# Order of three GpSimd subtractions, one first product and one small batch of matmuls in a fused attention and two-MLP kernel

## The chip, the cores and the metric

The kernel runs on one core of a Trainium2 chip. That core has TensorE (PE; its weight loads are shown apart, as PEld), VectorE (DVE), ScalarE (ACT), GpSimd (POOL) and SyncE (SP), which issues the DMAs. Each engine runs its own instructions in the order in which they stand, and waits on semaphores for the others. The metric is the time of one execution in microseconds on the device.

## The reference, cut to what matters

Three parts follow each other. With B = 4, H = 8, S = 512, 32 state rows per head and D = 64:

```python
a = softmax(x @ state.T / 8);   xread = a @ state
a2 = softmax(state @ x.T / 8);  sread = a2 @ x
x = concat(xread, sread)                      # 4 x 544 tokens, 512 wide
h = x @ w_in                                  # 512 -> 2048
x = softplus(h) @ w_out                       # 2048 -> 512
x = (silu(x @ w_gate) * (x @ w_val)) @ w_out2 # 512 -> 1536 -> 512
```

All of it is float32 in the reference; weights arrive as float64 words.

## The kernel before, in words

A float32 operand is split into a high float32r part (ACT) and a low part, whole minus high (POOL for most, DVE for some); every product is three matmuls: high by high, low by high, high by low (`mm3`, line 89). A weight tile of float64 words is first made float32 in steps: `size` (ACT, line 132), `head` (DVE, line 136), `tail` (two DVE instructions, lines 143 and 146).

The first MLP goes over the 2048 hidden columns in 4 chunks of 512. The attention read isn't formed: for each chunk c and batch b, `m` is the state times the chunk's w_in (`m_mm`, line 374, PE tile `pm`; high part on ACT, line 378; low part on DVE, line 92). A **unit** is (chunk, batch, 128 hidden columns): 16 units per chunk, 64 in all, numbered in that order, so that unit 9 is chunk 0, batch 2, tile 1. Each unit has these steps:

- first product `p1` (PE tile `ph_b_ft`, from `aT` and `m`, 6 matmuls),
- softplus twice on ACT: high part `h_b_ft` (line 404) and whole `C_b_ft` (line 407),
- low part `l_b_ft` = C - h on POOL (`g_low`, line 92),
- second product `p2` (PE tiles `py_b_0` to `py_b_3`, from `wo`, `h`, `l`: 4 times two matmuls with h and one with l).

`h`, `C` and `l` have three buffers each. The first product runs four units ahead of the second (LAG = 4). After the fourth unit of a batch, the four `py` go to `yacc` (DVE, and ACT in chunk 0). The state tokens (`s1`, line 505, PE tile `ps`: four matmuls with plain float32 operands) go beside this, and weights for the second MLP are converted in between.

Two things set the order. The table ORDER is a list of steps, written out by hand, for the attention and for the units up to the second product of unit 8 (`P8`) and the first of unit 12 (`p12`); there `p9` is a first product, `sp9` the two softplus, `gl9` the low part, `P9` a second product, `mh7` and `ml7` the high and low part of an `m`. From unit FIRST = 9 on a loop takes over: per step n it runs `p2` of unit n, the hooks of kind "pe", `p1` of unit n + 4, the softplus of unit n + 3 and the hooks of the other engines. M_STEPS gives the steps of a chunk at which the next chunk's four `m` batches are made; the "pe" hooks of a step also hold `s1`. The framework adds the waits and picks the buffers and PSUM banks. In the rows, a name such as `py_2_0` has lost its chunk number.

Of the kernel before, what the change touches and what calls it, by code (L numbers as in the profile page):

```python
# [31 lines left out]
)  # L32

FIRST = 9
# [3 lines left out]
def attention_moe_moe2_kernel(  # L38
# [44 lines left out]
    def bank(tag, name):  # L83
        return psum.tile([P, 512], F32, tag=tag, bufs=BUFS[tag], name=name)

    def mm3(o, a, b, first, last, **k):

        for i, (s, t) in enumerate(((0, 0), (1, 0), (0, 1))):
            nc.tensor.matmul(o, a[s], b[t], start=first and i == 0, stop=last and i == 2, **k)  # L89
# [322 lines left out]
    def p1(u):  # L412
        c, b, ft = u
        ps = bank("h", f"ph{c}_{b}_{ft}")
        f = slice(ft * P, (ft + 1) * P)
        for par in range(NPAR):
            mm3(
                ps, [mt[c, b, par][:, i, f] for i in range(2)], [aT[b, par][:, i, :] for i in range(2)],
                par == 0, par == NPAR - 1,
            )  # L420
        n = f"{c}_{b}_{ft}"
        sp[u] = Softplus(
            ps, work.tile([P, 512], F32, tag="C", name=f"C{n}"), work.tile([P, 512], F32R, tag="GH", name=f"h{n}")
        )

    def g_low(u):
        l = work.tile([P, 512], F32R, tag="GL", name="l%d_%d_%d" % u)
        low(nc.gpsimd, l, sp[u].g, sp[u].h)
        gT[u] = (sp[u].h, l)
# [5 lines left out]
    def p2(u):  # L435
        c, b, ft = u
        if ft == 0:
            for dt in range(KT):
                yps[dt] = bank("y", f"py{c}_{b}_{dt}")
        t = gT.pop(u)  # L440
        for dt in range(KT):
            mm3(yps[dt], [wo[c, ft].out[:, i, dt * P:(dt + 1) * P] for i in range(2)], t, ft == 0, ft == FT - 1)

    def y_add(c, b, dt):
        if (b, dt // 2) not in yacc:
            yacc[b, dt // 2] = slot([P, 2, 512], F32, "yacc", f"yacc{b}_{dt // 2}")
        v = yacc[b, dt // 2][:, dt % 2, :]
        if c == 0 and dt % 2:
            nc.scalar.activation(v, yps[dt], AF.Copy)
        elif c == 0:  # L450
            nc.vector.tensor_copy(v, yps[dt])
        else:
            nc.vector.tensor_tensor(out=v, in0=yps[dt], in1=v, op=ALU.add)  # L453
# [193 lines left out]


    LAG = 4
    M_STEPS = (9, 12, 15, 19)  # L650
    with tc.manual_schedule(engines={ENG.PE}):
        units = [(c, b, ft) for c in range(NCK) for b in range(B) for ft in range(FT)]
        NU = len(units)
# [3 lines left out]
        def first_load(key):  # L657
            if key == "st":
                nc.sync.dma_start(out=st, in_=st_d)
            elif key[0] == "w":  # L660
                win[0, int(key[1])] = piece_win(0, int(key[1]))
            elif key[0] == "o":
                wo[0, int(key[1])] = piece_wo(0, int(key[1]))
            else:
                (load_xt if key[0] == "x" else load_xn)(int(key[1]), int(key[2]))
# [11 lines left out]
        def do(names):  # L677
            for name in names.split():
                key = name.rstrip("0123456789")
                k = int(name[len(key):])  # L680
                if key in STEPS:
                    getattr(todo[k], STEPS[key])()
                elif key[0] in "io" and key[1:] in PIECE:
                    getattr((win if key[0] == "i" else wo)[0, k], PIECE[key[1:]])()
                elif key == "mm":
                    m_mm(0, k, 0, "m")
                    m_mm(0, k, 1, "y" if k < 2 else "h")
                elif key in BATCH:
                    BATCH[key](0, *divmod(k, 2))
                elif key == "st":  # L690
                    st_turn(k)
                elif key == "so":
                    st_out(k)
                elif key == "p":
                    p1(units[k])
                elif key == "sp":
                    sp[units[k]].high()
                    sp[units[k]].whole()
                elif key == "gl":
                    g_low(units[k])  # L700
                elif key == "P":
                    run(k, "load")
                    p2(units[k])
                elif key[0] == "y":
                    y_add(*units[k][:2], "abcd".index(key[1]))
                elif key == "jab":
                    win[1, k].size()
                elif key == "jhd":
                    win[1, k].head()
                elif key == "jtl":  # L710
                    win[1, k].tail()
# [3 lines left out]
        def at(n, kind, fn, *args):  # L715
            hooks.setdefault((n, kind), []).append((fn, args))

        def run(n, kind):
            for fn, args in hooks.get((n, kind), ()):
                fn(*args)  # L720
# [15 lines left out]
        for c in range(NCK):  # L736
# [5 lines left out]
            for i, (store, make, key) in enumerate(pieces):  # L742
                n, late = n0 + i // 2 * FT + i % 2, 2 - 2 * (i % 2)
# [3 lines left out]
            if c + 1 < NCK:  # L747
                for b, i in enumerate(M_STEPS):
                    at(n0 + i, "pe", m_pair, c + 1, b)
# [41 lines left out]
        with tc.manual_schedule(engines={ENG.DVE, ENG.SP, ENG.Activation, ENG.Pool}):  # L791
            for key in LOADS.split():
                first_load(key)
            for names in ORDER:
                do(names)
            room[0] = "m"
            for n in range(FIRST, NU):
                run(n, "load")
                if True:
                    u = units[n]  # L800
                    p2(u)
                    run(n, "pe")
                    if n + LAG < NU:
                        p1(units[n + LAG])
                nx = units[n + LAG - 1] if n + LAG - 1 < NU else None
                if nx:
                    sp[nx].high()
                    sp[nx].whole()
                last = u[2] == FT - 1
                run(n, "dve0")  # L810
                for dt in range(2) if last else ():
                    y_add(u[0], u[1], dt)
                run(n, "act")
                if nx:
                    g_low(nx)
                run(n, "pool")
                for dt in range(2, KT) if last else ():
                    y_add(u[0], u[1], dt)
                run(n, "dve1")
                run(n, "act1")  # L820
                run(n, "pool1")
            for n in range(NU, NU + FT + 1):
                for kind in ("act", "dve0", "pool"):
                    run(n, kind)
# [11 lines left out]
        for k, j in enumerate(range(len(EARLY), 3 * NF)):  # L836
            n, half = divmod(k, 2)
# [128 lines left out]
```

## Time and profile before

| what | value |
|---|---|
| time, median of 3 runs | 754.24 us (753.07 to 755.08) |
| the profiled execution: its own time | 753.34 us |
| its span, first to last instruction | 751.6 us |
| mean granted TensorE clock, share of full speed | 0.992 |
| PE busy | 722.4 us, 96% |
| DVE, POOL, ACT busy | 433.4 (58%), 385.1 (51%), 321.8 us (43%) |

The span is what the trace covers; 1.74 us of the profiled execution's time lie around it. A row of the timeline gives the start, the time to the last end, the engine, the line, and written tile <- read tiles; "[0.82 <-ACT m L378]" says how long the engine sat idle before it, and for whom. Consecutive matmuls overlap, so the pace of PE is read from start to start. "x16" in a row of a small or plain float32 batch counts records, which may be two for a matmul.

### The profile page before, as it was taken

To read this page: it belongs to the slowest core of one execution; us is meant where nothing else is said; L and a number is where in the kernel's file an instruction comes from. 1 tells how busy PE (TensorE), PEld (TensorE's weight loads), DVE (VectorE), ACT (ScalarE), POOL (GpSimd) and SP (SyncE) were. 2 spreads that over 40 slices of the span, in tenths; PEclk is the share of its full clock that TensorE was granted. 3 is DMA by queue.
4 is the path that set the end of the run, shared out by engine and by line. 5 is a ranking of instruction groups with operands and counts; after the bars stand their busy time and mean duration, and the time that the engine had idled before them with its cause. 6 is when DMAs were issued, how large, how long until landed. Compare 5 with 4: busy or idle time off the path is not lost.

```text
span 751.6 us, 9982 instructions
## 1 busy us (share of the span) xinstructions
PE 722.4 (96%) x3640; PEld 567.6 (76%) x3640; DVE 433.4 (58%) x605; ACT 321.8 (43%) x586; POOL 385.1 (51%) x352
## 2 busy tenths in 40 slices
PE   5699899999999999999999999999999999999997
PEld 1367567786777777788788788788888888888885
DVE  5984638878666866457576554554543333433344
ACT  3776335655454544534544444533442232223221
POOL 2467517786657765744775566574452232223222
PEclk9899999999999999999999999999999999999999
DMA  8920215555454535370398998877545746255402
GB/s 344 408 104 21 75 45 168 168 203 184 121 167 167 189 127 185 141 283 1 126 371 279 329 331 315 290 280 233 187 182 185 255 173 240 100 196 196 168 1 112
DMA packets 51073, 143.78 MB, mean 191 GB/s; under 512 B 5713, under 2 KB 18001, under 8 KB 51025
## 3 DMA queue, kind: packets, MB, share of 16 engines
q1 hardware_dynamic: 51024, 143.15, 54.2%
q8 instruction: 28, 0.46, 0.2%
q14 instruction: 21, 0.16, 0.1%
HBM read 107.22 MB, written 35.91 MB: 190 GB/s over the span
## 4 chain that ended last, share of the span: by engine, by line
PE 80%; DMA 6%; DVE 6%; ACT 3%; POOL 3%; issue 2%; SPq 1%; ACTq 0%; DVEq 0%; POOLq 0%
PE py L89 24%; PE po L89 16%; PE px L89 15%; PE ph L89 9%; PE pz L89 7%; DMA raw_gv<-in_moe_w_val_dram 4%; PE pt L89 3%; PE pm L374 2%; PE ps L505 2%; PE ps L89 1%; DMA gw<-gv_d 1%; POOL l L92 1%; POOL sums_gv L193 1%; DVE mx L273 1%; DMA st<-in_st_dram 1%
## 5 line engine op out<-in xcount | busy, mean ns | idle before, releaser
L89 PE MATMUL py<-h,wo 128*128 128x512 f32 x512 | 159.6, 392 | 2.3 <-DVE yacc L453 1.2
L92 POOL TENSOR_TENSOR l<-C,h 128x512 fp32r<-128x512 f32 x64 | 90.6, 1421 | 94.1 <-ACT C L407 81.2
L89 PE MATMUL po<-w,h 128*128 128x512 f32 x384 | 126.2, 391 | 0.0
L89 PEld LDWEIGHTS py<-h,wo 128*128 128x128 f32 x512 | 96.4, 189 | 23.7 <-POOL wo L92 1.9
L92 POOL TENSOR_TENSOR l<-cA,h 128x512 fp32r<-128x512 f32 x24 | 33.8, 1410 | 147.5 <-ACT h L574 147.5
L89 PE MATMUL ph<-aT,m 128*128 128x512 f32 x384 | 102.0, 400 | 1.8 <-ACT m L378 0.8
L89 PE MATMUL py<-l,wo 128*128 128x512 f32 x256 | 100.5, 393 | 2.5 <-POOL l L92 2.3
L404 ACT ACTIVATE h<-ph 128x512 fp32r<-128x512 f32 x64 | 38.2, 597 | 128.1 <-PE py L89 120.3
L89 PEld LDWEIGHTS ph<-aT,m 128*128 128x128 f32 x384 | 70.5, 188 | 27.9 <-issue 8.1
L595 DVE TENSOR_TENSOR oacc<-po,oacc 128x512 f32<-128x512 f32 x80 | 55.1, 690 | 60.8 <-PE po L89 60.5
L89 PEld LDWEIGHTS po<-w,h 128*128 128x128 f32 x384 | 72.1, 188 | 14.9
L89 PE MATMUL po<-w,l 128*128 128x512 f32 x192 | 74.9, 390 | 0.5 <-POOL l L92 0.5
L89 PE MATMUL px<-T_0s,gw 128*128 128x512 f32 x216 | 61.5, 393 | 3.7 <-ACT cA L884 2.1
L89 PE MATMUL px<-T_1s,gw 128*128 128x512 f32 x216 | 60.8, 389 | 0.0
L89 PEld LDWEIGHTS py<-l,wo 128*128 128x128 f32 x256 | 48.3, 189 | 13.5 <-POOL l L92 3.3
L89 PEld LDWEIGHTS px<-T_0s,gw 128*128 128x128 f32 x216 | 39.9, 188 | 14.3 <-ACT cA L884 3.3
L892 DVE TENSOR_TENSOR cA<-py,cA 128x512 f32<-128x512 f32 x24 | 16.6, 690 | 57.4 <-PE py L89 54.9
L574 ACT ACTIVATE h<-cA 128x512 fp32r<-128x512 f32 x24 | 15.1, 631 | 77.1 <-DVE cA L911 77.1
L89 PEld LDWEIGHTS px<-T_1s,gw 128*128 128x128 f32 x216 | 40.5, 188 | 8.6
L89 PEld LDWEIGHTS po<-w,l 128*128 128x128 f32 x192 | 36.1, 188 | 8.3 <-POOL l L92 1.0
L903 ACT ACTIVATE cC<-px 128x512 f32<-128x512 f32 x24 | 14.4, 598 | 62.9 <-PE px L89 59.4
L92 POOL TENSOR_TENSOR l<-cC,h 128x512 fp32r<-128x512 f32 x24 | 32.0, 1333 | 16.7 <-ACT h L574 16.7
(148 smaller groups left out, 1328.7 us busy)
## 6 DMA issues: line engine op xcount, KB each, us to landing
gw<-gv_d SPq DMA_DIRECT2D x96, 512.0 KB, 6.6
gv_d<-gv SPq DMA_DIRECT2D x24, 512.0 KB, 3.0
gv_d<-split_gv SPq DMA_DIRECT2D x24, 512.0 KB, 3.4
w<-w_d SPq DMA_DIRECT2D x24, 512.0 KB, 9.2
raw_win<-in_moe_w_in_dram SPq DMA_DIRECT2D x16, 512.0 KB, 7.1
raw_wo<-in_moe_w_out_dram SPq DMA_DIRECT2D x16, 512.0 KB, 4.0
raw_gv<-in_moe_w_gate_dram SPq DMA_DIRECT2D x48, 128.0 KB, 3.9
raw_gv<-in_moe_w_val_dram SPq DMA_DIRECT2D x48, 128.0 KB, 3.7
```

The source lines that it names most:

```text
L89: nc.tensor.matmul(o, a[s], b[t], start=first and i == 0, stop=last and i == 2, **k)
L92: eng.tensor_tensor(out=o, in0=whole, in1=high.bitcast(F32), op=ALU.subtract)
L193: nc.gpsimd.tensor_tensor(out=o, in0=x, in1=y, op=op)
L273: nc.vector.tensor_reduce(out=self.mine("mx", 1), in_=self.sc, op=ALU.max, axis=AX.X)
L374: nc.tensor.matmul(ps[k * NS:(k + 1) * NS, :], st[q, k, b, :], win[c, k].t[q, :], start=True, stop=True)
L404: nc.scalar.activation(self.h, self.ps, AF.Softplus)
L505: nc.tensor.matmul(ps, sw[:, kt, :], win[c, kt].t, start=kt == 0, stop=kt == KT - 1)
L574: nc.scalar.activation(h, src, AF.Copy)
L595: nc.vector.tensor_tensor(out=v, in0=ps, in1=v, op=ALU.add)
L892: nc.vector.tensor_tensor(out=c["A"], in0=y, in1=c["A"], op=ALU.add)
L903: nc.scalar.activation(c["C"], x, AF.Copy)
```

## The change: what it does

Three edits. In ORDER, the low part of unit 9 moves ahead (it stood last of the three), and the three low parts now stand as 9, 10, 11, where they stood as 11, 10, 9. `p12` leaves ORDER and is issued in the loop's first step, behind the second product of unit 9. The first number of M_STEPS goes from 9 to 10, for each of the three chunks that have a next one.

```diff
@@ ORDER
-    "sp9 ti7 p10 gl8 tu7 sp10 P7 jhd3 tu6 jtl3 ah6 ah7 al6 mm3 ya7 yd7 yb7 yc7 al7 p11 mh6 ml6 sp11 P8 mh7",
-    "gl11 ml7 jtl0 p12 gl10 jab2 jhd2 gl9 jtl2",
+    "sp9 ti7 p10 gl8 tu7 sp10 P7 jhd3 tu6 jtl3 ah6 ah7 al6 mm3 ya7 yd7 yb7 yc7 al7 p11 mh6 ml6 gl9 sp11 P8 mh7",
+    "gl10 ml7 jtl0 gl11 jab2 jhd2 jtl2",
@@ the loop's tables
-    M_STEPS = (9, 12, 15, 19)
+    M_STEPS = (10, 12, 15, 19)
@@ the loop
                     p2(u)
+                    if n == FIRST:
+                        p1(units[n + LAG - 1])
                     run(n, "pe")
                     if n + LAG < NU:
                         p1(units[n + LAG])
```

On POOL, behind the low parts of two `aT` (the attention weights of batch 3), the low parts of units 11, 10, 9 stood so before:

```order
L92 TENSOR_TENSOR aT_1_940<-t_1_911,aT_1_940 128x512
L92 TENSOR_TENSOR l_2_3_994<-C_2_3_967,h_2_3_968 128x512
L92 TENSOR_TENSOR l_2_2_1008<-C_2_2_907,h_2_2_908 128x512
L92 TENSOR_TENSOR l_2_1_1013<-C_2_1_872,h_2_1_873 128x512
L92 TENSOR_TENSOR l_3_0_1066<-C_3_0_1006,h_3_0_1007 128x512
```

And on POOL after the change, the same five:

```order
L92 TENSOR_TENSOR aT_1_940<-t_1_911,aT_1_940 128x512
L92 TENSOR_TENSOR l_2_1_972<-C_2_1_872,h_2_1_873 128x512
L92 TENSOR_TENSOR l_2_2_996<-C_2_2_907,h_2_2_908 128x512
L92 TENSOR_TENSOR l_2_3_1001<-C_2_3_967,h_2_3_968 128x512
L92 TENSOR_TENSOR l_3_0_1052<-C_3_0_1031,h_3_0_1032 128x512
```

The low part of unit 9 (`l_2_1`) moved from third to first, the one of unit 11 (`l_2_3`) from first to third.

On PE, from the end of unit 8's second product on, before (`ph_3_0` is the first product of unit 12, `py_2_0` here the second of units 9 and 10, `pm_0_0` and `pm_0_1` the next chunk's first `m` pair, the first `ps` chunk 0 of the state tokens, the second `ps` chunk 1):

```order
L89 MATMUL py_2_3_979<-l_2_0_909,wo_0_606 128x512
L89 MATMUL ph_3_0_999<-aT_0_938,m_3_0_969 128x512 x3
L89 MATMUL ph_3_0_999<-aT_1_940,m_3_1_992 128x512 x3
L89 MATMUL py_2_0_976<-h_2_1_873,wo_1_640 128x512 x2
L89 MATMUL py_2_0_976<-l_2_1_1013,wo_1_640 128x512
...
L374 MATMUL pm_0_0_1033<-t_win_0_745,st 32x512
...
L505 MATMUL ps_1043<-t_win_0_263,sw 128x512
...
L89 MATMUL ph_3_1_1049<-aT_0_938,m_3_0_969 128x512 x3
...
L89 MATMUL py_2_0_976<-h_2_2_908,wo_2_711 128x512 x2
...
L505 MATMUL ps_1087<-t_win_0_745,sw 128x512
```

And on PE after the change:

```order
L89 MATMUL py_2_3_981<-l_2_0_909,wo_0_606 128x512
L89 MATMUL py_2_0_978<-h_2_1_873,wo_1_640 128x512 x2
L89 MATMUL py_2_0_978<-l_2_1_972,wo_1_640 128x512
...
L89 MATMUL ph_3_0_1024<-aT_0_938,m_3_0_969 128x512 x3
L89 MATMUL ph_3_0_1024<-aT_1_940,m_3_1_994 128x512 x3
L505 MATMUL ps_1033<-t_win_0_263,sw 128x512
...
L89 MATMUL ph_3_1_1039<-aT_0_938,m_3_0_969 128x512 x3
...
L89 MATMUL py_2_0_978<-h_2_2_908,wo_2_711 128x512 x2
...
L374 MATMUL pm_0_0_1073<-t_win_0_745,st 32x512
...
L505 MATMUL ps_1083<-t_win_0_745,sw 128x512
```

The second product of unit 9 passed the first of unit 12, and the `m` pair went behind the second product of unit 10, straight ahead of the second `ps`. The number of matmuls is the same.

On DVE, in the middle of chunk 1, where the `m` pair of chunk 2 is now a step later (`m_0_0` and `m_0_1` are its low parts, `t_gv_1`, `t_wo_0` weight conversions, `yacc_0` the first sum of batch 2); before:

```order
L92 TENSOR_TENSOR m_0_0_1822<-pm_0_0_1800,m_0_0_1822 128x512
L92 TENSOR_TENSOR m_0_1_1824<-pm_0_1_1805,m_0_1_1824 128x512
L136 TENSOR_SCALAR t_gv_1_1834<-t_gv_1_1834 128x512
L143 SCALAR_TENSOR_TENSOR t_wo_0_1741<-raw_wo_0_1569,t_wo_0_1741 128x512
L146 SCALAR_TENSOR_TENSOR t_wo_0_1741<-raw_wo_0_1569,t_wo_0_1741 128x512
L143 SCALAR_TENSOR_TENSOR t_gv_1_1834<-raw_gv_1_1668,t_gv_1_1834 128x512
L146 SCALAR_TENSOR_TENSOR t_gv_1_1834<-raw_gv_1_1668,t_gv_1_1834 128x512
L453 TENSOR_TENSOR yacc_0_1140<-py_2_0_1745,yacc_0_1140 128x512
```

And after:

```order
L136 TENSOR_SCALAR t_gv_1_1820<-t_gv_1_1820 128x512
L143 SCALAR_TENSOR_TENSOR t_wo_0_1741<-raw_wo_0_1569,t_wo_0_1741 128x512
L146 SCALAR_TENSOR_TENSOR t_wo_0_1741<-raw_wo_0_1569,t_wo_0_1741 128x512
L143 SCALAR_TENSOR_TENSOR t_gv_1_1820<-raw_gv_1_1668,t_gv_1_1820 128x512
L146 SCALAR_TENSOR_TENSOR t_gv_1_1820<-raw_gv_1_1668,t_gv_1_1820 128x512
L92 TENSOR_TENSOR m_0_0_1867<-pm_0_0_1837,m_0_0_1867 128x512
L92 TENSOR_TENSOR m_0_1_1869<-pm_0_1_1842,m_0_1_1869 128x512
L453 TENSOR_TENSOR yacc_0_1140<-py_2_0_1745,yacc_0_1140 128x512
```

The two low parts moved behind five conversion instructions, and stand right ahead of the sums. Chunk 2 has the same piece once more. On ACT the two high parts move in the same way, behind the softplus of unit n + 3. The order of SP's DMAs is unchanged. The framework also picks other buffers: `t_win_2` (a w_in tile of chunk 1) now takes the place in SBUF of `t_win_0` of chunk 0, so that its first step on ACT, which stands ahead of the softplus of unit 12, waits until the first `ps` has read that tile.

## Rows read from the trace of the kernel before

**Rows 1.** What PE waited for, whole span: total us, times, longest

```profile
PE py L89 <- POOL l L92: 2.3, 1, 2.3
PE py L89 <- DVE yacc L453: 1.2, 1, 1.2
```

**Rows 2.** Timeline of PE: start us, us, engine line op, what, [idle before]

```profile
79.17 1.09 PE L374 MATMUL pm<-t_win,st 64*32 64x512 f32 x16
80.19 1.65 PE L89 MATMUL ph<-aT,m 128*128 128x512 f32 x6
81.68 0.62 PE L89 MATMUL py<-h,wo 128*128 128x512 f32 x2
...
84.41 0.84 PE L89 MATMUL ph<-aT,m 128*128 128x512 f32 x3
86.07 0.50 PE L89 MATMUL ph<-aT,m 128*128 128x512 f32 x1 [0.82 <-ACT m L378]
86.79 0.72 PE L89 MATMUL ph<-aT,m 128*128 128x512 f32 x2 [0.22 <-DVE m L92]
87.35 0.61 PE L89 MATMUL py<-h,wo 128*128 128x512 f32 x2
90.29 0.50 PE L89 MATMUL py<-l,wo 128*128 128x512 f32 x1 [2.32 <-POOL l L92]
...
94.07 1.36 PE L374 MATMUL pm<-t_win,st 64*32 64x512 f32 x16
95.36 3.70 PE L505 MATMUL ps<-t_win,sw 128*128 128x512 f32 x8
98.50 1.95 PE L89 MATMUL ph<-aT,m 128*128 128x512 f32 x6
100.28 0.62 PE L89 MATMUL py<-h,wo 128*128 128x512 f32 x2
...
103.02 3.59 PE L505 MATMUL ps<-t_win,sw 128*128 128x512 f32 x8
106.05 1.94 PE L89 MATMUL ph<-aT,m 128*128 128x512 f32 x6
...
110.55 1.52 PE L89 MATMUL ph<-aT,m 128*128 128x512 f32 x6
111.91 0.62 PE L89 MATMUL py<-h,wo 128*128 128x512 f32 x2
```

**Rows 3.** Timeline of POOL in the same place

```profile
80.82 2.56 POOL L92 TENSOR_TENSOR aT<-t,aT 128x512 fp32r<-128x512 f32 x2 [2.18 <-ACT aT L327]
85.60 4.64 POOL L92 TENSOR_TENSOR l<-C,h 128x512 fp32r<-128x512 f32 x3 [2.23 <-ACT C L407]
```

**Rows 4.** Timeline of ACT in the same place

```profile
75.47 0.59 ACT L407 ACTIVATE C<-ph 128x512 f32<-128x512 f32 x1
...
84.93 0.59 ACT L407 ACTIVATE C<-ph 128x512 f32<-128x512 f32 x1
85.41 0.60 ACT L378 ACTIVATE m<-pm 128x512 fp32r<-128x512 f32 x1
85.89 0.68 ACT L132 ACTIVATE t_win<-raw_win 128x512 f32<-128x512 f32 x1
```

**Rows 5.** Timeline of DVE in the same place

```profile
86.05 0.69 DVE L92 TENSOR_TENSOR m<-pm,m 128x512 fp32r<-128x512 f32 x1 [2.60 <-ACT m L378]
...
87.47 1.65 DVE L146 SCALAR_TENSOR_TENSOR t_win<-raw_win,t_win 128x512 int32<-128x512 int32 x1
```

**Rows 6.** Stretches: from:to, us, busy of each engine, then clock, DMA share, GB/s

```profile
90.29:94.07 3.78, 3.78 (x11) 2.51 (x11) 1.95 (x4) 0.24 (x1) 0.00 (x0) 0.63 0.60 193
...
95.36:111.91 16.55, 16.55 (x67) 11.03 (x60) 6.46 (x10) 5.27 (x10) 2.77 (x3) 1.00 0.09 32
```

**Rows 7.** Timeline of DVE in the middle of chunk 1

```profile
189.78 0.69 DVE L146 SCALAR_TENSOR_TENSOR t_gv<-raw_gv,t_gv 128x512 int32<-128x512 int32 x1
```

**Rows 8.** Timeline of PE in the middle of chunk 1

```profile
192.63 1.52 PE L89 MATMUL ph<-aT,m 128*128 128x512 f32 x6
```

## The prediction

> **What bounds the kernel now.** I read the busy shares first: PE is busy 96% of the span, the next engine 58%, so only what PE loses can be won. Then the list of PE's waits: after the start there are few, and the longest single one is 2.32 us for a low part on POOL; the next in the first MLP is 1.23 us for a sum on DVE [rows 1]. Then the timeline of PE around that wait. It shows one spoilt place, between 84.41, where the second product of unit 8 has ended, and 111.91, where the second product of unit 12 begins [rows 2]: 27.50 us.
>
> Three things go wrong there, one behind the other. The first product of unit 12 starts at 84.41, needs both `m` of batch 3, and has to wait in its middle for the second one: its high part is the ACT row at 85.41, its low part the DVE row at 86.05 [rows 4, 5]. PE stands idle 0.82 and 0.22 us, and the product takes 2.94 us, 84.41 to 87.35. Next, the second product of unit 9 starts at 87.35, does its two matmuls with `h`, and waits until 90.29 for the low part. POOL makes that one as the last of three, and the first of the three can't start before 85.60, because it is unit 11's and its C is the ACT row at 84.93 [rows 3, 4]. C of unit 9 was there since 75.47 plus 0.59 [rows 4]. Third, behind this idle time the granted clock is down: 0.63 on the mean from 90.29 to 94.07, 1.00 again from 95.36 on [rows 6]; of the two levels, 1.2 and 2.4 GHz, PE spends most of that stretch at the lower.
>
> **The change, part by part.** All moved instructions are still there, so PE's work is the same; the sum asks how long the same ten pieces take if none waits. At full clock, start to start [rows 2]: a second product 81.68 to 84.41, 2.73; a first product 110.55 to 111.91, 1.36; a `ps` batch 3.03 (103.02 to 106.05) or, behind an `m` pair, 3.14 (95.36 to 98.50); a first product behind a `ps`, 1.78 (98.50 to 100.28); a second product up to a `ps`, 2.74 (100.28 to 103.02); an `m` pair 1.02 (79.17 to 80.19), for which I take 1.1, with a tenth for the change of form ahead of it. In the new order:
>
> 2.73 (second of 9) + 1.36 (first of 12) + 3.03 (`ps`) + 1.78 (first of 13) + 2.74 (second of 10) + 1.1 (`m` pair) + 3.14 (`ps`) + 1.78 (first of 14) + 2.74 (second of 11) + 1.36 (first of 15) = 21.76 us.
>
> Against 27.50 this is **5.74 us less**. By place: first of 12 2.94 - 1.36 = 1.58; second of 9 (87.35 to 94.07) 6.72 - 2.73 = 3.99; the rest, 0.17, on the `m` pair and rounding. In the 3.99, the wait is 90.29 - 87.35 - 0.46 = 2.48 (0.46 is the two matmuls with `h`, a sixth of 2.73), and the lower clock 1.51.
>
> Does each piece really find its inputs? In the trace's own times:
>
> *Second of 9.* It would start at 84.41 and want its low part 0.46 later, at 84.87. POOL ends the two `aT` at 80.82 + 2.56 = 83.38 and stood idle for 2.23 us then [rows 3]; the low part of unit 9 has its C and takes its place. Two such subtractions took 2.56, so one takes 1.28 and ends at 84.66: 0.2 us in time. The three of before took 4.64, so 1.55 each; with that the low part ends at 84.93, and PE loses 0.1. I take the 1.28. In these 1.28 us DVE does not convert weights: it stood idle 2.60 us ahead of 86.05 [rows 5], while the three of before ran beside conversions such as the 1.65 us row at 87.47.
>
> The Trainium skill, page "SBUF — State Buffer", section "SBUF: two separate sides", says that GpSimd and a DVE instruction with two SBUF inputs use one port pair as an exclusive lock, so that one blocks the other. By that rule 1.28 holds here and the sum stays at 5.74; if the slow rows have another cause, 1.55 holds and the sum is 5.64. The trace agrees with the rule as far as it goes: the slow subtractions and the slow conversion are beside each other, the 1.28 ones beside idle DVE.
>
> *First of 12*, now at 87.14: its last input, the low part of `m`, is ready at 86.05 + 0.69 = 86.74. *`ps`*, at 88.50: old inputs. *Second of 10*, at 93.31, and *of 11*, at about 102: their low parts are POOL's next two, done by 87.5 even at 1.55 each.
>
> *The `m` pair*, at 96.05: new is that `t_win_2` waits on ACT for the first matmul of `ps`, about 89.3 instead of 85.89, and with it the softplus of unit 12 behind it. Its 0.68 on ACT and three DVE instructions, at the 1.65 of [rows 5] each, end near 95; near 92 at 0.69. Either is before 96.05, and C of unit 12 is wanted as low part only at the second product of unit 12, near 106. So this costs nothing, by 1 us at the worst. If the cover were gone, PE would wait at the pair for what is missing.
>
> *Later chunks.* Moving the pair a step adds no PE work (0.0, at most 0.1 each, for the neighbours that `ps` and the pair get). New is the wait of DVE's two `m` low parts behind five conversions: the last of those ends at 189.78 + 0.69 = 190.47, the first low part 0.69 later at 191.2 [rows 5, 7]; the first product that takes over its PSUM bank starts at 192.63 [rows 8]. It is covered by 1.4 us. Behind the two, the four sums start about 1 us later than before, and the second product that needs their banks comes more than a first product (1.36) later. Twice the same; cost nothing, bounds 0 to 1 us.
>
> *Buffers and banks of the later phases* are dealt out anew, so the 1.23 us wait [rows 1] may vanish or double: -1.2 to +1.2, taken as 0. Nothing waits on a clock of its own there: what PE finds late is tied to earlier PE work, so the 5.74 should arrive at the end.
>
> Sum: 753.34, the profiled execution (span 751.6 and 1.74 around it), minus 5.74 gives 747.6. The median of the runs is 0.90 above the profiled one, so the time is 754.24 - 5.74 = **748.5 us**.
>
> **The rivals.**
>
> *A: one idle place is only moved.* The low part is 0.2 us in time, no more; if POOL or ACT is late there, or the pair waits for `t_win_2`, PE stands still once, and a clock drop may follow. Price: a wait of about 1 us with a drop like the one shown (1.51), 2.5 us, so a gain of 3.2: 751.0. For it: the thin margin. Against: every input but that one is there by 1 us or more. Chance 0.12.
>
> *B: the gain is given back later.* DVE and POOL work on the weights through chunk 1, and the 1.23 us wait for a DVE sum shows that they are close to PE. If that chain ran at its own pace, PE would arrive 5.74 earlier and wait: 754.2, no change. Against: its instructions stand in queues behind softplus and sums that wait for PE. Chance 0.07.
>
> *C: slower.* The two `m` low parts behind the conversions become late in chunks 1 and 2, and hold up first the bank of a first product, then the four sums and the second products of the next batch. The margin is 1.4 us; the last conversion, at 0.69, takes 1 us of it if it grows to 1.65. A loss begins when the two parts end more than 1.4 + 2.9 = 4.3 us later than worked out, at both places (2.9 is half of 5.74); at 5.5 us later it is 2 x 4.1 = 8.2 against 5.74, which gives 756.7. Against: no row shows conversions growing by that much. Chance 0.04.
>
> A gain larger than the sum, by the vanished 1.23 wait: 747.3; chance 0.10. The forecast itself: 0.67.
>
> **How the numbers follow.** Two runs of this kernel that differ by under 0.3%, 2.3 us, can't be told apart; so faster is below 752.0. The forecast, the larger gain and A are there: 0.67 + 0.10 + 0.12, less 0.02 of A's tail, 0.87. Same: B and 0.01 of that tail, 0.08. Slower: C and the other 0.01, 0.05. The range runs from 746.5 (larger gain, and 0.8 for the spread of the runs) to 751.3 (A), and leaves out B and C.
>
> **What would show it.** In the new profile PE's list of waits has no 2.3 us for POOL and no `m` wait at a first product; the clock is 1.00 from the second product of unit 8 to that of unit 12; that stretch is near 21.8 us; the first of POOL's three low parts begins right at the end of the `aT` pair. Wrong would be a PE wait at the first `pm` pair or in front of a `ph` of batch 3 in chunks 1 and 2, or a wait for a DVE sum above 2 us.

## The result, and the profile after

The changed kernel takes 746.98 us (median, runs from 746.17 to 748.9), the kernel before in the same session 753.65: a ratio of 0.991, 95% interval 0.989 to 0.9929, 0.9% faster, more than the 0.3% that can be told apart. The profiled execution took 746.57 with a span of 744.8 and a mean clock of 0.999.

PE's list of waits, whole span (us in total, times, longest). The 2.3 us for POOL that stood in [rows 1] is gone; the sum on DVE is still there. The wait of a first product for `m` is not the one of [rows 2]: it stands at 37.35, in the opening, ahead of all that the change moves.

```profile
PE sc L267 <- DMA st<-in_st_dram: 7.2, 1, 7.2
...
PE py L89 <- DVE yacc L453: 1.2, 1, 1.2
...
PE ph L89 <- DVE m L92: 0.7, 1, 0.7
```

The timeline of PE that answers to [rows 2], each piece's first row (start us, us, engine line operation, tiles):

```profile
84.86 0.62 PE L89 MATMUL py<-h,wo 128*128 128x512 f32 x2
...
87.61 1.52 PE L89 MATMUL ph<-aT,m 128*128 128x512 f32 x6
88.97 3.59 PE L505 MATMUL ps<-t_win,sw 128*128 128x512 f32 x8
92.00 1.94 PE L89 MATMUL ph<-aT,m 128*128 128x512 f32 x6
93.78 0.62 PE L89 MATMUL py<-h,wo 128*128 128x512 f32 x2
...
96.59 1.09 PE L374 MATMUL pm<-t_win,st 64*32 64x512 f32 x16
97.61 3.70 PE L505 MATMUL ps<-t_win,sw 128*128 128x512 f32 x8
...
106.63 0.61 PE L89 MATMUL py<-h,wo 128*128 128x512 f32 x2
```

The second product of unit 8 ends at 84.86 and the second of unit 12 starts at 106.63: 21.77 us, where it was 27.50. Of the same stretch the view by stretches says that PE is busy in every part of it and that its clock is at the upper level (from:to, length, then busy us of PE, PEld, DVE, ACT, POOL, then clock, DMA share, GB/s), against 0.63 in [rows 6]:

```profile
84.86:88.97 4.11, 4.11 (x19) 3.38 (x18) 2.31 (x3) 1.58 (x3) 2.71 (x3) 1.00 0.00 0
88.97:106.63 17.66, 17.66 (x75) 11.02 (x74) 9.09 (x14) 7.42 (x14) 2.78 (x3) 1.00 0.29 90
```

POOL, as in [rows 3], and DVE's last step of the window `t_win_2`, for which ACT's first step now waits for `ps`:

```profile
81.25 2.56 POOL L92 TENSOR_TENSOR aT<-t,aT 128x512 fp32r<-128x512 f32 x2 [2.23 <-ACT aT L327]
83.76 3.81 POOL L92 TENSOR_TENSOR l<-C,h 128x512 fp32r<-128x512 f32 x3
```

```profile
90.03 0.67 ACT L132 ACTIVATE t_win<-raw_win 128x512 f32<-128x512 f32 x1 [3.56 <-PE ps L505]
```

```profile
91.92 0.69 DVE L146 SCALAR_TENSOR_TENSOR t_win<-raw_win,t_win 128x512 int32<-128x512 int32 x1
```

The low parts follow the `aT` pair without a pause and take 1.27 each (3.81 / 3) instead of 1.55. The first is done at about 85.05 (83.76 plus 1.27 and rounding) and wanted at 85.32 (84.86 plus 0.46, the two matmuls with `h`).

Where the 6.8 us between the two spans come from: the second product of unit 8 ends 0.45 later (PE's first wait, for the load of `st`, is 7.2 us instead of 6.4, and part of that is made up in the opening), the stretch gives 5.73, from there to the second MLP nothing changes (243.97 us after, 244.04 before), and the second MLP gives about 1.4, which the prediction did not have.

### The profile page after: what moved, and what is told of

Read it like the earlier page. It is cut to its first block, busy times and chain, and to the rows that moved or that the text cites. A ratio compares the mean times of both kernels' runs of the same rounds, so it can differ in the third digit from the quotient of the medians.

```text
span 744.8 us, 9985 instructions
## 1 busy us (share of the span) xinstructions
PE 718.5 (96%) x3640; PEld 566.9 (76%) x3640; DVE 427.9 (57%) x605; ACT 321.5 (43%) x586; POOL 384.4 (52%) x352
## 4 chain that ended last, share of the span: by engine, by line
PE 82%; DVE 6%; DMA 4%; ACT 3%; POOL 3%; issue 2%; SPq 0%; ACTq 0%; DVEq 0%; POOLq 0%
PE py L89 24%; PE px L89 16%; PE po L89 16%; PE ph L89 10%; PE pz L89 7%; PE pt L89 3%; DMA gw<-gv_d 2%; PE ps L505 2%; PE pm L374 2%; DMA raw_gv<-in_moe_w_val_dram 2%; PE ps L89 1%; DMA st<-in_st_dram 1%; POOL sums_gv L193 1%; POOL gv L92 1%; DVE mx L273 1%
```

## Experiments

Eight kernels ran, one of them the changed kernel again. "The stretch" is always the one above, from the end of unit 8's second product to the start of unit 12's. Stretches come from one profile each, times are medians of 4 to 12 runs. Ratios are to the kernel before in the same session: 753.65 for the changed kernel, 754.0 for the low parts only, the first product of 12 only, the old `m` pair and the old first product of 12, and 753.49 for the other four, which ran on another chip than these four.

| kernel | stretch, us | second of unit 12 to second MLP, us | time, median, us | ratio to before, 95% |
|---|---|---|---|---|
| before | 27.50 | 244.04 | 753.65 | |
| changed | 21.77 | 243.97 | 746.98 | 0.989 to 0.9929 |
| changed, again | 21.78 | 242.80 | 747.58 | 0.9903 to 0.9939 |
| low parts only | 23.36 | 243.98 | 748.61 | 0.9917 to 0.9948 |
| first product of 12 only | 28.87 | 244.02 | 755.94 | 1.0006 to 1.0033 |
| m pair only | 28.40 | 243.98 | 752.98 | 0.9984 to 1.0012 |
| changed, old m pair | 23.40 | 242.76 | 748.99 | 0.9925 to 0.9961 |
| changed, old first product of 12 | 23.35 | 243.96 | 749.48 | 0.9924 to 0.9959 |
| changed, low part of 9 as second | 22.89 | 242.81 | 748.07 | 0.9914 to 0.9953 |
| changed, sums first | 21.74 | 242.03 | 745.55 | 0.9872 to 0.9908 |

**Low parts only.** From the changed kernel, two edits are taken back:

```diff
-    "gl10 ml7 jtl0 gl11 jab2 jhd2 jtl2",
+    "gl10 ml7 jtl0 p12 gl11 jab2 jhd2 jtl2",
-    M_STEPS = (10, 12, 15, 19)
+    M_STEPS = (9, 12, 15, 19)
-                    if n == FIRST:
-                        p1(units[n + LAG - 1])
```

> Only the order of the low parts (unit 9, 10, 11) is changed; the first product of unit 12 stays ahead of the second of unit 9, and the first m pair of a chunk stays where it was. Theory 1 (the waits add up, each has its own cause): the 2.3 us wait for POOL and the lower clock behind it go, the 1.58 us that the first product of unit 12 loses to its waits for m stay. Gain about 4.0 us, so near 749.7, and the stretch from the end of the second product of unit 8 to the second of unit 12 takes 23.3 to 23.7 us; the m pair may wait up to 1 us for its window. Theory 2 (the waits for m alone are enough to bring the clock down): the 2.48 us wait goes, but a stretch at the lower clock stays and keeps about 1.5 us: gain 2.5, near 751.2.

PE's timeline and the view by stretches of this kernel:

```profile
85.05 0.84 PE L89 MATMUL ph<-aT,m 128*128 128x512 f32 x3
86.72 0.49 PE L89 MATMUL ph<-aT,m 128*128 128x512 f32 x1 [0.82 <-ACT m L378]
87.44 0.73 PE L89 MATMUL ph<-aT,m 128*128 128x512 f32 x2 [0.23 <-DVE m L92]
88.01 0.62 PE L89 MATMUL py<-h,wo 128*128 128x512 f32 x2
```

```profile
88.01:90.84 2.83, 2.83 (x14) 2.07 (x12) 2.73 (x6) 0.04 (x1) 0.00 (x0) 1.00 0.28 75
```

The waits for both `m` are those of before to 0.01 us, and right behind them the clock is at its upper level. So the long wait for the low part, not these two, goes with the fall of the clock: theory 1. The stretch of 23.36 is where theory 1 put it; the median, 748.61, lies 1.1 below the 749.7 expected. The stretch is 1.59 longer than in the changed kernel, where the prediction's term for the first product of unit 12 is 1.58.

**First product of unit 12 only.** The low parts are made in the old order:

```diff
-    ... ml6 gl9 sp11 P8 mh7",
-    "gl10 ml7 jtl0 gl11 jab2 jhd2 jtl2",
+    ... ml6 sp11 P8 mh7",
+    "gl11 ml7 jtl0 gl10 jab2 jhd2 gl9 jtl2",
-    M_STEPS = (10, 12, 15, 19)
+    M_STEPS = (9, 12, 15, 19)
```

> Only the first product of unit 12 is moved behind the second of unit 9; the low parts are made in the old order (11, 10, 9). Theory 1: the second product of unit 9 starts at about 84.4, wants its low part at 84.9 and gets it at about 90.3: one wait of 5.4 us in place of 0.82 + 0.22 + 2.3. The first product of unit 12 then waits for nothing. The work between (1.36) no longer lies inside the wait, so the stretch is 1.4 us longer than before, and with a longer time at the lower clock up to 3: 755 to 756.7, slower than before. Theory 2 (the move of the first product is what brings the gain by itself): 1.6 us faster than before, 752.

```profile
86.16 0.61 PE L89 MATMUL py<-h,wo 128*128 128x512 f32 x2
92.02 0.80 PE L89 MATMUL py<-l,wo 128*128 128x512 f32 x1 [5.24 <-POOL l L92]
```

```profile
92.02:95.17 3.15, 3.15 (x7) 2.50 (x8) 1.95 (x4) 0.00 (x0) 0.00 (x0) 0.50 0.52 183
95.17:95.99 0.82, 0.82 (x5) 0.69 (x3) 0.00 (x0) 0.00 (x0) 0.00 (x0) 0.85 0.85 269
```

The stretch is 1.37 longer than before, and the time 0.19% above it (0.06 to 0.33): a small loss, clear of zero by its interval but below the 0.3% used above, and no gain of 1.6. The stretch is at the lower end of what theory 1 expects, the median of 755.94 inside its range. The product that is moved away had filled part of the wait. The wait is more than twice that of [rows 2] and the lower clock costs the same: 3.15 us at 0.50 and 0.82 at 0.85 are 1.7 us lost, and before it is 3.78 at 0.63 [rows 6], 1.4, with a rest on the `m` pair, which takes 1.29 (94.07 to 95.36) for 1.02: 1.7 too.

**m pair only.** Low parts and the first product of unit 12 stand as before; only `M_STEPS` begins with 10.

> Only the first m pair of each chunk comes a step later; low parts and the first product of unit 12 as in the kernel before. Theory 1: the pair costs PE the same in either place, and the first product of unit 12 and the second of unit 9 wait as before; the stretch takes 27.4 to 27.6 us and the time is that of the kernel before, 753.5 to 754.3. Theory 2 (the later pair alone gives the 1.4 us that the changed kernel gained in the second MLP): 752.4.

```profile
89.89 0.79 PE L89 MATMUL py<-l,wo 128*128 128x512 f32 x1 [2.30 <-POOL l L92]
```

```profile
89.89:94.32 4.43, 4.43 (x10) 3.47 (x11) 0.00 (x0) 0.00 (x0) 0.00 (x0) 0.50 0.30 112
94.32:97.77 3.45, 3.45 (x10) 1.50 (x8) 1.21 (x3) 1.98 (x4) 0.00 (x0) 0.88 0.00 0
```

No change in the time that the runs show; theory 2's gain of 1.4, a ratio of 0.998, lies just outside the interval. The stretch missed the expectation by 0.9: behind nearly the same wait (2.30) the clock stayed down for longer, 4.43 x 0.50 + 3.45 x 0.12 = 2.6 us lost instead of 1.7. So the price of the clock behind this wait varies. The runs of this kernel go from 751.33 to 756.57, those of the changed kernel from 746.17 to 749.07 over both sessions; that the wider spread comes from the clock is not shown.

**Changed, old m pair.**

```diff
-    M_STEPS = (10, 12, 15, 19)
+    M_STEPS = (9, 12, 15, 19)
```

> The changed kernel with the first m pair of each chunk one step earlier again. Theory 1 (this part of the change only clears the place of the pair): the pair stands right behind the first product of unit 12, at about 89, and the window that it reads is not finished by then; PE waits 1 to 3 us there, with a drop of the clock behind it in the worst case: 748 to 751. In the later chunks nothing changes. Theory 2 (the step is without effect): 747, and the stretch takes 21.8 us as in the changed kernel. Theory 3 (the later step of the pair is also what gained the 1 us in the second MLP of chunk 1): the part from the second product of unit 12 to the end takes 639.7 as before, not 638.2.

```profile
87.08 1.52 PE L89 MATMUL ph<-aT,m 128*128 128x512 f32 x6
88.53 1.05 PE L374 MATMUL pm<-t_win,st 64*32 64x512 f32 x4
90.15 1.08 PE L374 MATMUL pm<-t_win,st 64*32 64x512 f32 x12 [0.57 <-DVE t_win L146]
91.16 1.12 PE L505 MATMUL ps<-t_win,sw 128*128 128x512 f32 x2
```

Theory 1: the pair has caught up with its window and takes 2.63 (88.53 to 91.16) for 1.02, and the view by stretches has the clock at 1.00 there. The later step is worth 1.63 (23.40 against 21.77) with both other edits in place. Alone it was worth nothing, and with the low parts alone nothing either: 23.36 in the kernel with the low parts only, 23.35 in the next one, which has the later step besides. The shorter way to the second MLP, 242.76, is looked at below.

**Changed, old first product of unit 12.** `p12` is back in ORDER and out of the loop.

> The changed kernel with the first product of unit 12 ahead of the second of unit 9 again; low parts and m pair as changed. Theory 1: the first product of unit 12 starts at about 84.9 and waits 0.8 + 0.2 us for the two m again, 2.9 us in place of 1.36; the clock stays at its upper level: 1.6 us slower than the changed kernel, 748.6. Theory 2 (1 us of idle time is enough to bring the clock down): 3 us slower, 750. Theory 3 (its wait is covered by something else late, so that it costs nothing): 747.0.

The same 0.82 and 0.23, the clock at 1.00 from 88.62 to 91.37 by the view of stretches, and a stretch of 23.35: 1.58 more, theory 1. The median of 749.48 lies 0.9 above the 748.6 expected.

**Changed, low part of unit 9 as second.** `gl10` ahead of `gl9`.

> The changed kernel, but POOL makes the low part of unit 10 ahead of that of unit 9. Theory 1 (a low part takes 1.27 on POOL): that of unit 9 ends 1.25 later, and PE, which had 0.3 us to spare, waits about 1.0 us at the second product of unit 9; a single microsecond does not bring the clock down, so the stretch takes 22.8 us, and the time is 1.0 above the repeat of the changed kernel. Theory 2 (any wait just there brings the clock down): 2.5 above. Theory 3 (the place in POOL's row isn't what counts): no difference.

```profile
85.57 0.61 PE L89 MATMUL py<-h,wo 128*128 128x512 f32 x2
87.04 0.50 PE L89 MATMUL py<-l,wo 128*128 128x512 f32 x1 [0.86 <-POOL l L92]
```

The stretch is 1.1 longer and the clock stays at 1.00: theory 1. The medians, 748.07 and 747.58, are only 0.5 apart where 1.0 was expected, and their runs overlap; the verdict rests on the trace.

**Changed, again.**

> The changed kernel once more, unchanged, for a second profile. Theory 1 (the 1.4 us that it gained in the second MLP is chance, not the change): the way from the first product of the second MLP to its last first-matrix product, 375.5 in the first profile of the changed kernel and 377.0 in that of the kernel before, comes out elsewhere between 375.4 and 377.8. Theory 2 (it belongs to the changed kernel's buffers and banks): 375.4 to 375.7 again. The stretch takes 21.8 in either.

The first product `pz` of the second MLP and the last product `px` with `T_0s`, in the first and in the second profile of the changed kernel:

```profile
350.60 0.84 PE L89 MATMUL pz<-T_0s,gw 128*128 128x512 f32 x3
...
726.14 0.84 PE L89 MATMUL px<-T_0s,gw 128*128 128x512 f32 x3
```

```profile
349.43 0.84 PE L89 MATMUL pz<-T_0s,gw 128*128 128x512 f32 x3
...
726.42 0.84 PE L89 MATMUL px<-T_0s,gw 128*128 128x512 f32 x3
```

375.54 and 376.99 us: theory 1. The other kernels lie from 376.0 to 377.7, before at 376.95. Two profiles of one kernel differ by as much, so the 1.4 us there are no part of the change; what made the first profile faster is open.

The same profile has a second surprise: no wait for a DVE sum. In the changed kernel's first profile, DVE, POOL and PE stand so (three views; the first DVE row is the step `head`, line 136, which the recorded expectation below calls a size step):

```profile
165.97 1.52 DVE L136 TENSOR_SCALAR t_gv<-t_gv 128x512 int32<-128x512 int32 x1
167.42 2.47 DVE L453 TENSOR_TENSOR yacc<-py,yacc 128x512 f32<-128x512 f32 x4
```

```profile
165.92 1.29 POOL L92 TENSOR_TENSOR l<-C,h 128x512 fp32r<-128x512 f32 x1 [1.75 <-ACT C L407]
```

```profile
168.15 0.74 PE L89 MATMUL py<-h,wo 128*128 128x512 f32 x2 [1.23 <-DVE yacc L453]
```

and in the second profile of the same kernel:

```profile
165.95 0.42 DVE L136 TENSOR_SCALAR t_gv<-t_gv 128x512 int32<-128x512 int32 x1
166.28 2.48 DVE L453 TENSOR_TENSOR yacc<-py,yacc 128x512 f32<-128x512 f32 x4
```

```profile
165.93 1.58 POOL L92 TENSOR_TENSOR l<-C,h 128x512 fp32r<-128x512 f32 x1 [1.78 <-ACT C L407]
```

DVE's `head` step and POOL's low part start within 0.05 us of each other. Once the `head` step takes 1.52 and the low part 1.29, once 0.42 and 1.58: one of the two has its own time, the other its own and most of the first one's. PE's 1.2 us hang on which of them waits. In the table's third column all kernels up to here fall into 244.0 or 242.8, and the changed kernel has both, so the program alone does not set which. The nine profiles up to here sort without exception: the six at 244.0 have a `head` row of 1.52 to 1.55 here, the three at 242.8 one of 0.42. POOL's row starts first in all nine, by 21 to 51 ns in the six and by 14 to 17 ns in the three.

**Changed, sums first.** The idea follows from these rows: the sums that PE waits for go ahead of the `head` step.

```diff
-                run(n, "dve0")
                 for dt in range(2) if last else ():
                     y_add(u[0], u[1], dt)
+                run(n, "dve0")
```

> The changed kernel, with the first two sums of a batch issued on DVE ahead of the size steps (and m low parts) of that step; PE's, POOL's and SP's rows stay as they are. In the changed kernel a size step of 0.42 us took 1.52 there, since it came 0.05 us behind the start of a low part on POOL, and the sums and PE stood behind it. Theory 1 (DVE waits for POOL's whole instruction only in that form of operation, and the sums in their place don't): the 1.23 us wait for a DVE sum goes, nothing else moves: 1.2 below the repeat of the changed kernel. Theory 2 (the sums are caught by the same low part): the wait shrinks by 0.4 at most and the time stays. Theory 3 (the gain is lost again in the second MLP, where DMA is at 0.9): the stretch from the first product of the first MLP to the second MLP is 1.2 shorter and the time is the same.

```profile
165.23 1.28 DVE L453 TENSOR_TENSOR yacc<-py,yacc 128x512 f32<-128x512 f32 x2
166.43 0.42 DVE L136 TENSOR_SCALAR t_gv<-t_gv 128x512 int32<-128x512 int32 x1
```

```profile
164.81 1.68 POOL L92 TENSOR_TENSOR l<-C,h 128x512 fp32r<-128x512 f32 x1 [1.37 <-PE py L89]
166.44 1.56 POOL L92 TENSOR_TENSOR w<-t_w,w 128x512 fp32r<-128x512 f32 x1
```

The two sums, 0.64 each, run at their own pace beside a low part. (The low part's 1.68 holds some 0.4 in which DVE's conversion from 164.62 to 165.31 was still running.) The wait is gone, and the way to the second MLP takes 242.03: 1.94 less than in the first profile of the changed kernel, 0.77 less than in the second, which had no such wait either. So one profile without the wait would not show that the edit removed it; the order of the rows does, since the sums no longer stand behind the `head` step. Of both differences 0.39 comes near 115, where a first product of the changed kernel waits for a low part of `m` on DVE that now starts 0.3 earlier. The rest falls on this batch's products: 0.38 against the second profile, 1.55 with the listed wait of 1.23 against the first. The median, 745.55 (744.56 to 745.93), is 2.0 below the changed kernel in the same session, and no run of the one reaches the other. Theory 1 has the wait right, but expected 1.2 and nothing else to move. This kernel is the fastest version that ran; theories 2 and 3 are out.

## Why the prediction was right

*The sum.* Ten pieces at full clock were forecast at 21.76 and take 21.77. By place: the first product of unit 12 takes 1.36 (87.61 to 88.97), as forecast. Its loss of 1.58 came back as 1.59 and 1.58 in the two kernels that undo this part. The low parts alone took 4.14 off the stretch (27.50 to 23.36), where the prediction's term is 3.99. The second product of unit 9 takes 2.75 (84.86 to 87.61), forecast 2.73. The `m` pair takes 1.02, forecast 1.1.

*The low part in time.* Forecast 0.2 us ahead, by 1.28 for one; measured 1.27, and 0.27 ahead. The kernel with the low part in second place shows how thin that is: one subtraction later, and PE waits 0.86. The 1.28, and not the 1.55, was right.

One reading behind it was not: the prediction has DVE idle beside the two `aT` subtractions of 1.28. In the trace of before, DVE copies sums out of PSUM and makes a low part of `m` there:

```profile
80.76 1.28 DVE L451 COPY yacc<-py 128x512 f32<-128x512 f32 x2
82.75 0.69 DVE L92 TENSOR_TENSOR m<-pm,m 128x512 fp32r<-128x512 f32 x1 [0.71 <-ACT m L378]
```

Neither has two inputs in SBUF, as the conversions beside the slow subtractions have, so the choice of 1.28 stands. The Trainium skill, page "SBUF — State Buffer", section "SBUF: two separate sides", on which the prediction weighed this, says too that whichever of GpSimd and the DVE instruction starts first holds the pair for its whole instruction. The Trainium skill, section "Who interferes with whom" of that page, counts `tensor_scalar`, the `head` step's operation, among those that can take the pair. The durations at 165.9 agree in both orders: 1.52 is the `head` step's 0.42 and most of the low part's 1.29, and 1.58 the low part's 1.29 and most of the 0.42. The recorded starts do not show the order, since POOL's row starts first in either; a lead of 14 to 17 ns on POOL still let DVE go first.

*The lower clock.* Forecast: gone with the long wait. It is, in each kernel without that wait, also where 0.82 + 0.23 or 0.86 us of idle time remain. Its price, 1.51 and some rounding, fits the profiled execution of before, but in the kernel with the `m` pair only nearly the same wait cost 2.6.

*The `m` pair.* Forecast: `t_win_2` ready between 92 and 95, wanted at 96.05. It is ready at 92.6 (91.92 + 0.69) and wanted at 96.59; no wait. The kernel with the pair a step earlier shows what this cover is worth.

*Later chunks.* Forecast to cost nothing, with the first of the two low parts of `m` done 1.4 us ahead of the first product that takes over its bank. After, in the places of [rows 7] and [rows 8], the two run from 184.93 to 186.21, so the first is done near 185.6, and the first product starts at 187.30 without a wait, 1.7 us later:

```profile
184.93 1.28 DVE L92 TENSOR_TENSOR m<-pm,m 128x512 fp32r<-128x512 f32 x2
```

```profile
187.30 1.52 PE L89 MATMUL ph<-aT,m 128*128 128x512 f32 x6
```

PE's list of waits has none at this place in chunk 2 either. That rules out rival C. Rival B, a gain given back, is ruled out by the third column of the table: from the second product of unit 12 to the second MLP, the changed kernel is as fast as before, and in the second MLP it is no slower (375.54 and 376.99 against 376.95). Rival A's wait did not come. Its price was too high: with the low part of unit 9 in second place the wait does come, 0.86, and costs 1.1, not 2.5, since no fall of the clock follows. Its argument that every other input is there by 1 us or more does not fit the prediction's own numbers: the last `m` for the first product of unit 12 was due at 86.74 for 87.14, 0.4 ahead, and came at 87.19 (86.50 + 0.69) for 87.61, again 0.4.

*The size.* 748.5 was forecast, 746.98 and 747.58 were measured; against the kernel before of the same session that is 6.67 and 5.91 less, where 5.74 was forecast. The stretch was right to 0.01 (that near is in part luck: pieces are off by up to 0.08 either way), so the difference lies outside of it. For the profiled execution 747.6 was forecast and 746.57 came, and that 1.0 is the 1.4 us in the second MLP, which the second profile did not repeat, less 0.45 at the start. Besides, the forecast took the clock's price from one execution, and it is at the lower end of the three prices seen (1.7, 1.7 and 2.6). The bounds of 1.2 either way on buffers and banks had the right size but the wrong reason: the 1.23 us wait comes or goes between two runs of one kernel, and is not set by how the buffers are dealt out. So the larger gain, a rival at 747.3, does come: in one of the two profiles of the changed kernel.

## What to carry to other kernels

When PE waits, read when each input of the waiting instruction was ready to be made, not only when it was made: here C of unit 9 was there at 76.06 [rows 4], and only its place in POOL's row kept the low part until 90. Edits to an order can depend on each other: of these three, one alone gained most (4.14 us of the stretch), one alone lost 1.37, one alone gained nothing, and together they were worth 5.73. And profile a kernel twice before a wait of a microsecond is put down to an edit.

## What the runs showed of the hardware

A `head` step on DVE and a subtraction on POOL (both 128x512) that start within 0.05 us of each other cost 0.42 and 1.58 or 1.52 and 1.29, and which it is differs between two profiles of one kernel. In nine profiles DVE went first where its row started 14 to 17 ns behind POOL's, and waited where it started 21 to 51 ns behind. A sum on DVE that reads PSUM is not touched: 0.64 each beside a low part on POOL.

The lower clock came in every kernel with a single wait of 2.3 us or more in this place and in none with 1.1 us of listed idle time or less; a wait of 5.24 did not cost more of it than one of 2.32, and two waits of 2.3 cost 1.7 and 2.6. Why these two differ is open. In the opening of the kernel the clock falls too, and not at a fixed place: from 30.5 to 34.2 it is 1.00 in the first profile of the changed kernel and 0.78 in the second.
